# Decay attention with a softplus feed-forward on one core: one block's second product moved behind the others, two pools of PSUM banks joined, q loaded in natural order, another order of instructions

## The chip, the cores and the metric

One core of one Trainium2 chip runs the whole program. The metric is device time in microseconds; lower is better. Engines are called PE (TensorE, with PEld for its weight loads), DVE (VectorE), ACT (ScalarE), POOL (GpSimd) and SP (SyncE, which issues nearly all transfers).

## What is computed

Cut to what matters, the reference is

```python
# q, k, v: (8, 8, 576, 64); f: (8, 8, 576); w_in: (512, 2048); w_out: (2048, 512)
cum = cumsum(log(clip(f, 1e-4, 1)), -1)
scores = q @ k.T / 8 + cum[..., :, None] - cum[..., None, :]      # causal
attn = softmax(scores)                                           # sum + 1e-9
x = (attn @ v) -> (4608 tokens, 512)
h = x @ w_in
out = softplus(h) @ w_out                                        # (4608, 512)
```

All inputs and the output are float32 (the weights reach the kernel as 64-bit words).

## The kernel before

**Precision.** A float32 product is made of three products in a faster format (F32R): each operand is split into a high and a low part, and high times high, high times low and low times high are summed in PSUM. So each operand costs a copy (the high part, `hi_part` or `high`, on ACT or DVE) and a subtraction (the low part, `lo_part` or `low`, on DVE or POOL). The first 14 attention jobs and the first two feed-forward blocks (`plain`) use float32 matmuls directly.

**Work.** There are 70 attention jobs: 14 plain ones for batch 0, and 56 of the split form, one for each head of batches 1 to 7 (`attention`, with `load`, `prepare`, `stat_tile`, `weights`, `output`, `finish`). The 4608 tokens go through the feed-forward in blocks: two of 128 tokens, one of 256, four of 512 (`ffn_block`, blocks 3 to 6; block 6 is tokens 2048 to 2559), and two late blocks of 1024 (`super_blocks`). A 512-token block makes its first product in 16 steps of 12 matmuls (`up_part`, L1506, into a PSUM bank of the tag `h`), softplus on ACT and a split (`gate`), and its second product with 2 of its 4 token tiles at once (`down_part`), the gate's values for the other two tiles going to HBM (`g_d`) and coming back for `second`, the block's tail. Both run through `products`, L1580, and sum up in two banks of the tag `acc`. Tail and normal part are 96 matmuls each.

**Late blocks.** After the last attention job the two late blocks run with a seven-product scheme over quarters of the operands (products P1 to P7 with sums of quarters, instead of eight). First all first products (L2050, 42 matmuls of 512 columns for each of 8 pairs of feature columns and each block); their softplus goes unsplit to HBM (`raw_d`). Then all second products in sets (`down_set` loads, sums and splits; `down_products`, L2387, 42 matmuls of 256 columns for a set; `down_out` joins the seven results). There are 2 blocks x 4 x 4 = 32 sets.

**Order.** Nothing is ordered by hand. Each operation is entered into a `Plan` with its possible engines and a cost for each, what it waits for, and the tags of the buffers that it takes. `Plan.run` then picks, among the next 700 entries, the one that could start first by these costs, less a bonus for its kind (`SOONER`), on the engine that would end it first, with a bias for kind and engine (`RATHER`); this gives each engine its queue. Feed-forward steps are dealt out between the attention units of each job in even shares (`run_ffn`, `share`), so that they last until `REST` = 4 jobs after the last one; with `PAIR` = 1.4 a share is saved up until that much work is due. An operation that is not `loose` takes a buffer of a tag only as the first in that tag's queue. Eight PSUM banks are divided as `att` 4, `h` 2, `acc` 2. `fill_gap` puts dummy matmuls into gaps of PE's plan until the first `acc` bank is taken.

**Operands of an attention job.** `load` brings q and k twice, for the two halves of the partitions. q is brought with its 64-element groups in reverse order (`last_first`), 256 bytes a piece; k as it lies. `prepare` casts them into the operand tile T (L329, ACT or DVE) and subtracts for the low parts (L931). `set_rows` writes constant rows into each of the two T tiles once the plain jobs have read them for the last time.

**Handover.** The late blocks take over the buffers of the attention: operand splits go into the tiles `raw`, T, `vhl`, `ph`, `pl`, `p` and `xl`, sums of weights into `xh` (`place["sums"]`). `xh` and `xl` belong to the running 512-token block until its last `up_part`. The steps of block 6's tail that are left are placed between the first steps of the late blocks (`kept_units`, `left`).

## Time and profile before

| | us |
|---|---|
| median of 3 runs | 1126.86 (1124.36 to 1128.87) |
| the profiled execution | 1123.38 |
| its span on the core | 1121.6 |

The profile is of one execution, which was 3.48 us faster than the median of the three runs. Its span runs from the first to the last recorded instruction; 1.78 us of its time lie around the span.

### The profile page before, as it was taken

The page shows a single profiled execution, that of the slowest core. Times are in us where ns is not written, and L with a number is a line of the kernel's source. Part 1 is how long each engine was busy: PE and PEld are TensorE (multiplying, and loading weights), DVE is VectorE, ACT ScalarE, POOL GpSimd, SP SyncE. Part 2 cuts the span into 40 slices and gives each one's busy share as a digit, 9 for nine tenths or more (in the row PEclk, how much of TensorE's full clock was granted, in tenths as well). Part 3 has the DMA queues.
Part 4 walks back from the last instruction along what each step waited for, and adds up shares of the span by engine and source line. Part 5 has one row for each costly group of instructions (what it writes and reads, how often), then busy time and mean ns, then how long its engine had stood idle before and what let it go on. Part 6 is the DMA issues. An engine that isn't in the chain of part 4 may idle for free.

```text
span 1121.6 us, 21642 instructions
## 1 busy us (share of the span) xinstructions
PE 1101.8 (98%) x6764; PEld 950.3 (85%) x6764; DVE 883.7 (79%) x2445; ACT 811.0 (72%) x2014; POOL 471.6 (42%) x426
## 2 busy tenths in 40 slices
PE   9999999999999999999999999999999999999998
PEld 7777688888888888888888888888888788999998
DVE  7887799887776777878788877886865997998773
ACT  7888789878887888878888888786554665544441
POOL 3423556656663456644655445553000245002111
PEclk9999999999999999999999999999999999999999
DMA  8877676545565566565657646645776776443431
GB/s 224 255 221 229 192 223 182 161 145 176 149 193 173 164 184 194 150 196 153 187 158 204 196 143 203 176 147 161 235 226 189 238 209 196 137 137 122 147 123 57
DMA packets 220866, 200.54 MB, mean 179 GB/s; under 512 B 86384, under 2 KB 189072, under 8 KB 220752
## 3 DMA queue, kind: packets, MB, share of 16 engines
q1 hardware_dynamic: 220728, 199.15, 59.7%
q8 instruction: 53, 0.87, 0.3%
q14 instruction: 61, 0.50, 0.1%
q10 hardware_dynamic: 24, 0.02, 0.0%
HBM read 141.17 MB, written 57.84 MB: 177 GB/s over the span
## 4 chain that ended last, share of the span: by engine, by line
PE 81%; DVE 11%; DMA 3%; ACT 3%; issue 1%; SPq 0%; POOL 0%; DVEq 0%; ACTq 0%; POOLq 0%
PE acc L1580 17%; PE h L1506 14%; PE b L1118 7%; PE late_E L2387 7%; PE late_E L2050 6%; PE o L1265 6%; PE s L976 3%; PE s L977 3%; PE h L1485 2%; PE s L971 2%; PE late_B L2387 2%; PE late_D L2050 2%; PE late_D L2387 2%; PE late_C L2387 2%; PE late_A L2387 2%; PE late_C L2050 1%
## 5 line engine op out<-in xcount | busy, mean ns | idle before, releaser
L1025 ACT ACTIVATE pb<-s,negm 128x288 f32<-128x288 f32 (+5 forms) x272 | 143.9, 531 | 54.4 <-DVE negm L1018 52.6
L981 DVE CUSTOM_DVE_ANT_0 s<-s,cmask 128x448 f32<-128x448 f32 (+6 forms) x320 | 138.2, 435 | 53.5 <-PE b L1118 26.7
L1550 POOL TENSOR_TENSOR gl<-e,gh 128x512 fp32r<-128x512 f32 x72 | 94.7, 1316 | 102.2 <-DVE gh L329 42.9
L931 POOL TENSOR_TENSOR T<-k,T 64x576 fp32r<-64x576 f32 x56 | 80.4, 1436 | 118.4 <-ACT T L329 67.2
L329 ACT CAST ph<-b 64x128 fp32r<-64x128 f32 x224 | 101.8, 490 | 23.7 <-PE b L1118 22.5
L1140 DVE TENSOR_TENSOR pl<-b,ph 128x512 fp32r<-128x512 f32 x168 | 106.4, 662 | 15.0 <-ACT ph L329 14.0
L976 PE MATMUL s<-T 128*128 128x192 f32 (+1 forms) x336 | 99.7, 304 | 4.3 <-ACT p L1025 2.4
L977 PE MATMUL s<-T 68*128 68x192 f32 (+1 forms) x336 | 98.0, 295 | 0.0
L1506 PE MATMUL h<-xh,wl 128*128 128x512 f32 (+1 forms) x320 | 89.5, 374 | 0.0
L1265 PE MATMUL o<-ph,vhl 128*128 128x512 f32 x336 | 87.9, 299 | 0.4 <-DVE pl L1140 0.2
L931 POOL TENSOR_TENSOR T<-q,T 64x576 fp32r<-64x576 f32 x56 | 81.6, 1457 | 15.6 <-ACT T L329 9.9
L1506 PE MATMUL h<-xh,wih 128*128 128x512 f32 (+1 forms) x320 | 81.6, 377 | 0.0
L1118 PE MATMUL b<-halves,pb 128*128 128x128 f32 x512 | 79.8, 273 | 0.0
L1506 PE MATMUL h<-xl,wih 128*128 128x512 f32 (+1 forms) x320 | 79.4, 370 | 0.0
L329 ACT CAST T<-k 128x576 fp32r<-128x576 f32 x112 | 75.2, 673 | 3.8 <-PE s L976 1.7
L903 POOL TENSOR_TENSOR vhl<-vr,vhl 128x384 fp32r<-128x384 f32 x56 | 58.3, 1041 | 44.7 <-DVE vhl L329 19.7
L976 PEld LDWEIGHTS s<-T 128*128 128x128 f32 (+1 forms) x336 | 60.7, 181 | 14.7 <-ACT p L1025 3.1
L1580 PE MATMUL acc<-woh_dt_float32r,gh 128*128 128x512 f32 x176 | 71.9, 409 | 0.0
L1055 DVE TENSOR_SCALAR pb<-pb,rsum 128x576 f32<-128x576 f32 (+2 forms) x86 | 69.8, 823 | 1.1
L1265 PEld LDWEIGHTS o<-ph,vhl 128*128 128x128 f32 x336 | 63.5, 189 | 7.8 <-DVE pl L1140 1.0
L1265 PE MATMUL o<-pl,vhl 128*128 128x512 f32 x224 | 68.5, 345 | 1.0 <-DVE pl L1140 0.8
L1580 PE MATMUL acc<-woh_dt_float32r,gl 128*128 128x512 f32 x176 | 69.3, 394 | 0.0
(747 smaller groups left out, 3358.3 us busy)
## 6 DMA issues: line engine op xcount, KB each, us to landing
wl<-wil_d SPq DMA_DIRECT2D x40, 512.0 KB
raw_d<-e SPq DMA_DIRECT2D x64, 256.0 KB
q<-in_qkT SPq DMA_DIRECT2D x112, 144.0 KB
k<-in_qkT SPq DMA_DIRECT2D x112, 144.0 KB
vr<-in_vR SPq DMA_DIRECT2D x64, 160.0 KB
x_d<-x SPq DMA_DIRECT2D x28, 288.0 KB
g_d<-gh SPq DMA_DIRECT2D x56, 128.0 KB
g_d<-gl SPq DMA_DIRECT2D x56, 128.0 KB
```

What stands on the lines that cost most here:

```text
L329: (e.tensor_copy if hasattr(e, "tensor_copy") else e.copy)(out, in_)
L931: e.tensor_sub(t[rows, i, :], st[x][rows], tb[rows, j, :])
L976: e.matmul(o, qA[:, S - end : S - q0], kA[:, a:z], start=True, stop=False)
L977: e.matmul(o, qB[0:ST, S - end : S - q0], kB[0:ST, a:z], start=False, stop=True)
L981: e.tensor_tensor_reduce(out=box["o"], in0=box["o"], in1=cmask[0:n_q, right - w : right], scale=-0.125, scalar=m0 if i else 3.0e38, op0=AL ...
L1025: e.activation(o, box["o"], AF.Softplus, bias=m1, scale=-1.0, accum_out=acc)
L1118: e.transpose(box["ps"][0 : x.shape[1], at : at + one.shape[1]], x, one)
L1140: e.tensor_sub(box["l"], box["ps"][:, 0:w], box["h"].bitcast(F32))
L1265: e.matmul(boxes[gi]["ps"][0:m, a:z], st["vhl"][:, c, 0:m], pbox[which][:, o : o + z - a], start=gi in fresh and which == "h", stop=gi == ...
L1506: e.matmul(o, l, r, start=m == 0, stop=m == 11)
L1580: e.matmul(st["acc", tt], l, r[fc], start=first and m == 0, stop=last and m == 2,)
L2387: e.matmul(like(o, y), x, y, start=q == 0 and f_ == 0 and m == 0, stop=q == NQ - 1 and f_ == 1 and m == 2,)
```

## The change

- `LATE_DOWN = (6,)`: block 6 no longer makes its second product in the middle. Its softplus goes unsplit to HBM (`whole_keep` into `raw_m`); its gate's split, its 96 + 96 matmuls of L1580, its g_d traffic and its tail are gone. Instead the late stage makes it in 2 x 4 = 8 more sets, ahead of the other 32. The shares of `run_ffn` count 12 instead of 24 matmul groups for such a block.
- `acc` and `att` become one tag `att` with six banks; the two sums of a 512-token block take two of them while they last. The dummy matmuls take one until the first up-projection.
- q is loaded in natural order, 2304 bytes a piece; the reversal of its groups is done by the casts and subtractions of `prepare`, which read q in reverse.
- `PAIR` = 0, many new values in `SOONER` (the plain jobs have their own, marked " early") and `RATHER`, some costs of the planner changed (a shift costs 0.11 us more, the cast of v is counted as fast on DVE, some operations count as using a port that DVE and POOL share).
- `HYB` = 8 lets a number of plain jobs run in the split form from 6 + 8 = 14 on. The first split job is number 14 before as well, so with this value no job changes its form. `set_rows` for one T tile waits for the scores of one plain job instead of two.

```diff
-PLAIN = 0
+HYB = 8
+LATE_DOWN = (6,)
-PAIR = 1.4
+PAIR = 0.0
...
 RATHER = {
-    ("attention.prepare.<lambda>", "ACT"): -1.44,
+    ("attention.prepare.<lambda>", "ACT"): 0.75,
...
-                if "acc" in op.takes:
+                if op is self.stop:
                     self.fill = None
...
-    BUFS = dict(T=2, att=4, h=2, acc=2, fe=4, ph=3, pl=3, ph64=2, gh=LAG + 1, gl=LAG + 1, xh=1, xl=1,
+    BUFS = dict(T=2, att=6, h=2, fe=4, ph=3, pl=3, ph64=2, gh=LAG + 1, gl=LAG + 1, xh=1, xl=1,
+    raw_m = dpool.tile([max(1, len(LATE_DOWN)), 2, 2, WIDE // 256, 2, P, NFP // 2, P], F32, name="raw_m")
...
                 for r in (0, 64):
-                    out = st["q"][r : r + 64].rearrange("p (n t) -> p n t", t=64)
-                    e.dma_start(out=out, in_=last_first(qkT[b, :, heads[0], 0]))
+                    e.dma_start(out=st["q"][r : r + 64, 0 : S - qs], in_=qkT[b, :, heads[0], 0, qs:])
...
             def high(e, i, x, rows):
-                copy(e, t[rows, i, :], st[x][rows])
+                if x == "q":
+                    copy(e, blocks(t[rows, i, 0:nq]), last_first(st[x][rows, 0:nq]))
+                else:
+                    copy(e, t[rows, i, 0:S], st[x][rows])
...
-            if number < nplain + 2:
-                set_rows(number % 2, T0_end[2 * (number % 2)] + T0_end[2 * (number % 2) + 1])
+            if number < nfirst + HYB + 2:
+                set_rows(number % 2, T0_end[number % 2])
...
             a = add(on_act(512, psum=True), raw, after=st["ups"][-1:], takes=("gh",) if plain else ("fe",))
             give("h", [a])
+            if i in LATE_DOWN:
+                m = LATE_DOWN.index(i)
+
+                def whole_keep(e):
+                    for odd in range(2):
+                        to = raw_m[m, odd, u % 2, :, u // 8, :, u // 2 % 4]
+                        e.dma_start(
+                            out=to.rearrange("k p n -> p k n"),
+                            in_=box["g"][:, TB * odd : TB * odd + TB].rearrange("p (k n) -> p k n", n=P),
+                        )
+
+                d = add_dma(whole_keep, 256, 2, after=[a])
+                give("fe", [add(NO_ENGINE, mark, after=[d])])
+                for odd in range(2):
+                    kept_at[NSUPER + m, odd, u] = d
+                return
...
-            tags = ["acc"] * len(tiles)
+            tags = ["att"] * len(tiles)
...
-            downs.append([(down_t, lambda u=u, k=k: down_part(u, k)) for k in range(nk)])
+            downs.append([(down_t, lambda u=u, k=k: down_part(u, k)) for k in range(nk) if not raw_only])
         tail = []
-        if ahead < ntile:
+        if raw_only:
+            pass
+        elif ahead < ntile:
...
-        sets = [(s, k, q) for s in range(NSUPER) for k in range(SUPER // 256) for q in range(NQ)]
+        sets = [
+            (NSUPER + m, k, q) for m in range(len(LATE_DOWN)) for k in range(WIDE // 256) for q in range(NQ)
+        ]
+        sets += [(s, k, q) for s in range(NSUPER) for k in range(SUPER // 256) for q in range(NQ)]
...
-            later = sum(NFC * on_pe(WIDE, 24).cost for x in ready_at.values() for _ in x)
+            later = sum(
+                NFC * on_pe(WIDE, 12 if i in LATE_DOWN else 24).cost for x in ready_at.values() for i in x
+            )
```

## Rows read from the trace of the kernel before

**Rows 1.** The page's first two parts: busy time, share of the span and instructions of each engine; then TensorE's busy tenths and its granted clock (PEclk, tenths of full speed) in 40 equal slices of the span.

```profile
span 1121.6 us, 21642 instructions
...
PE 1101.8 (98%) x6764; PEld 950.3 (85%) x6764; DVE 883.7 (79%) x2445; ACT 811.0 (72%) x2014; POOL 471.6 (42%) x426
...
PE   9999999999999999999999999999999999999998
...
PEclk9999999999999999999999999999999999999999
```

**Rows 2.** Busy time by stage: stretch, its length, busy us (and instructions) of PE, PEld, DVE, ACT and POOL, granted clock, DMA share, GB/s. The stages are: plain float32 attention and feed-forward; the first jobs of the split form; the middle; the handover; the first products of the two late blocks (two rows); their second products (two rows).

```profile
0.00:137.00 137.00, 132.21 (x898) 100.92 (x898) 105.41 (x330) 112.54 (x272) 53.53 (x83) 1.00 0.78 226
137.00:330.00 193.00, 186.45 (x1155) 161.16 (x1155) 164.55 (x495) 160.87 (x432) 119.43 (x94) 1.00 0.59 174
330.00:770.00 440.00, 439.68 (x2553) 378.14 (x2552) 343.89 (x1067) 361.09 (x969) 236.59 (x189) 1.00 0.59 174
770.00:800.00 30.00, 30.00 (x159) 25.32 (x158) 21.08 (x46) 16.98 (x39) 2.84 (x2) 1.00 0.63 199
800.00:860.00 60.00, 60.00 (x267) 49.69 (x266) 36.80 (x68) 28.63 (x51) 1.12 (x1) 1.00 0.75 220
860.00:960.00 100.00, 96.42 (x436) 78.53 (x435) 86.75 (x154) 63.12 (x128) 38.63 (x39) 1.00 0.73 214
960.00:1100.00 140.00, 139.87 (x1166) 139.66 (x1165) 120.03 (x280) 66.41 (x128) 19.48 (x20) 1.00 0.42 131
1100.00:1122.00 22.00, 17.13 (x143) 16.93 (x142) 5.15 (x12) 1.35 (x3) 0.00 (x0) 1.00 0.07 25
```

**Rows 3.** The chain that ended last, in order of time (start us, us, what): a run of the middle form's second product (L1580), a run of the late first product (L2050), and three successive sets of the late second product (L2387).

```profile
786.37 8.21 PE acc L1580 x36
...
806.82 9.52 PE late_E L2050 x42
...
1020.65 1.44 PE late_E L2387 x12
...
1025.69 1.44 PE late_E L2387 x12
...
1030.73 1.44 PE late_E L2387 x12
```

**Rows 4.** Who made PE wait between 137 and 330 us: engine line waited for, us in total, times, the longest.

```profile
PE b L1118 <- ACT p L1025: 2.3, 5, 0.5
PE s L976 <- ACT p L1025: 2.2, 2, 1.9
PE o L1265 <- DVE pl L1140: 1.1, 2, 0.8
```

**Rows 5.** Groups of instructions by line over the whole span: busy us, mean ns of one, and after the second bar the engine's idle time before them.

```profile
L1550 POOL TENSOR_TENSOR gl<-e,gh 128x512 fp32r<-128x512 f32 x72 | 94.7, 1316 | 102.2 <-DVE gh L329 42.9 <-issue 13.6 <-DMA k<-in_qkT 12.4
...
L329 ACT CAST T<-k 128x576 fp32r<-128x576 f32 x112 | 75.2, 673 | 3.8 <-PE s L976 1.7 <-DMA k<-in_qkT 0.9 <-issue 0.6
...
L329 ACT CAST T<-q 128x576 fp32r<-128x576 f32 x56 | 37.9, 676 | 0.5 <-DMA q<-in_qkT 0.4
...
L329 DVE CAST gh<-e 128x512 fp32r<-128x512 f32 x61 | 27.7, 454 | 14.3 <-ACT e L325 7.1 <-POOL vhl L903 3.5 <-DMA vr<-in_vR 1.7
...
L2641 PE MATMUL fill<-cmask 128*128 128x128 f32 x44 | 6.9, 282 | 0.0
```

**Rows 6.** A stretch of the middle in which TensorE is never idle (columns as in Rows 2), and two pieces of the chain that stand at the same place of two jobs, two jobs apart.

```profile
395.00:625.00 230.00, 230.00 (x1347) 198.44 (x1346) 183.09 (x564) 189.99 (x511) 134.62 (x108) 1.00 0.60 178
...
433.63 1.49 PE o L1265 x10
...
456.64 1.49 PE o L1265 x10
```

**Rows 7.** The handover, in order of time: the last up-projection of block 6 (L1506), the last attention product (L1265), the first late product (L2050) and block 6's last second products (L1580) on PE; then on DVE the splits of the late weight sums (L1977) and of the operand T4 (late_xl, L1840).

```profile
758.37 1.07 PE L1506 MATMUL h<-xl,wih 128*128 128x512 f32 x4
...
786.04 0.33 PE L1265 MATMUL o<-ph,vhl 128*128 128x320 f32 x1
...
794.42 0.39 PE L2050 MATMUL late_A<-late_raw,wih 128*128 128x512 f32 x1
...
795.78 0.39 PE L1580 MATMUL acc<-woh_dt_float32r,gh_6b 128*128 128x512 f32 x1
...
787.75 0.76 DVE L1977 TENSOR_TENSOR late_xh<-p,late_xh 128x256 fp32r<-128x256 f32 x2
...
800.10 0.69 DVE L1840 TENSOR_TENSOR late_xl<-late_T,late_xl 128x512 fp32r<-128x512 f32 x1
```

**Rows 8.** Packets of all transfers (the DMA view), the queue that carries them, the issues of the q loads with their duration on the queue (ns min/median/max) from the view of the tile q, and one piece of the chain.

```profile
DMA packets 220866, 200.54 MB, mean 179 GB/s; under 512 B 86384, under 2 KB 189072, under 8 KB 220752
...
q1 hardware_dynamic: 220728, 199.15, 59.7%
...
L886 SPq DMA_DIRECT2D q<-in_qkT x112: 626/645/1491, 95.7 to 743.1; - x112
...
113.10 7.18 DMA sto<-in_w_out
```

**Rows 9.** The memsets of the constant rows of the operand tiles T (line 466, called from set_rows): engine, count, ns min/median/max, first and last start; and what their engine waited for.

```profile
L466 POOL MEMSET T<- x4: 571/571/572, 89.9 to 109.7; 4x576 f32 x4
...
  PE s L971: 1.5, 2
```

More of the change, by code (lines that the diff above doesn't have):

```diff
@@ new lines @@
+    "attention.load.k early": -0.11,
+    "attention.load.q": 0.7,
+    "attention.load32.qk early": 4.58,
+    "attention.load32.rows early": 5.34,
+    "attention.load_quad.<lambda> early": 3.74,
+    "attention.load_v.v early": 0.28,
+    "attention.prepare.decay_rows": 2.88,
+    "attention.split_v.v_hi": -0.39,
+    "attention.split_v.v_hi early": -0.21,
+    "attention.split_v.v_lo": -0.72,
+    "attention.stat_tile.scores": 0.08,
+    "attention.stat_tile.scores early": 2.28,
+    "attention.stat_tile.sums early": 5.04,
@@ new lines @@
+    "attention.stat_tile.weight early": -0.17,
+    "attention.weights.hi_part": 0.04,
+    "attention.weights.keep early": 0.15,
+    "attention.weights.spread": 3.08,
+    "attention.weights.spread early": -0.43,
+    "attention.weights.turn": 0.09,
+    "decay.load early": 3.08,
+    "ffn_block.gate.hi_part": -0.29,
+    "ffn_block.gate.keep": -0.98,
+    "ffn_block.gate.lo_part": -0.38,
+    "ffn_block.gate.raw": -0.54,
+    "ffn_block.gate.raw early": -0.3,
+    "ffn_block.gate.whole_keep": 5.1,
@@ L116 @@
[L116 to L124 removed]
+    ("attention.finish_stats.scale", "ACT"): -1.26,
@@ new lines @@
+    ("ffn_block.gate.lo_part", "POOL"): 0.21,
+    ("load_f64.sign early", "ACT"): -1.9,
+    ("put_out.<lambda>", "ACT"): -0.38,
+    ("split_w_out.hi_part early", "ACT"): 0.46,
+    ("split_w_out.hi_part early", "DVE"): 0.51,
+    ("super_blocks.down_set.split.high", "DVE"): 1.33,
+    ("super_blocks.lay_sums.<lambda>", "POOL"): 0.16,
+    ("super_blocks.lay_sums.low", "POOL"): 1.93,
+    ("super_blocks.lay_w.split.hi", "ACT"): 1.54,
+    ("super_blocks.lay_w.split.hi", "DVE"): 0.19,
+    ("super_blocks.lay_x.less.go", "DVE"): 0.6,
```

230 lines of the change are left out of this document (123 added, 107 removed).

## The prediction, made before the changed kernel was run

> **What bounds the kernel now.** I read the page's first parts first: PE is busy for 98% of the span, in every slice but the last, and its granted clock is full throughout, so the clock is no part of the argument [rows 1]. A busy PE is not yet PE at its peak, so the next view is the table of stages [rows 2]: between 330 and 860 us PE is never idle for more than 0.3 us, and between 960 and 1100 us it rests 0.1 us. Its idle time is 4.8 us before 137 us, 6.6 us from 137 to 330, 3.6 us from 860 to 960 and 4.9 us at the very end, 20 us in all; 6.9 us of dummy matmuls at the start are counted as busy [rows 5]. So the kernel is bound by the sum of PE's work. An edit can gain in two ways only: less work for PE, or less of those 20 + 7 us. An edit that relieves another engine, or a transfer, gains nothing where PE has no gap.
>
> **Part one: block 6's second product moves to the late stage.** It removes 2 x 96 = 192 matmuls of L1580. A run of 36 takes 8.21 us, 0.228 us each [rows 3], so 192 take 43.8 us; by the late first product's pace (9.52 us for 42, 0.227) they would be 43.5. It adds 8 sets. Sets follow each other in 5.04 us (1020.65, 1025.69, 1030.73), which is 42 matmuls at the 0.120 us that 12 in 1.44 us give [rows 3]; the stretch 960 to 1100 has 1166 matmuls in 139.9 us, the same 0.120 [rows 2]. Eight sets: 40.3 us. Net **-3.5 us** (bounds -3.2 and -3.5). The seven-product scheme saves an eighth of the columns, but half of that is lost, because 256 columns in 0.120 us are slower for a column than 512 in 0.228; PEld is busy for 139.7 of those 140 us, so the weight load has become as long as the matmul it should hide behind [rows 2]. DVE is busy for 86% of that stretch, 4.3 us of each 5.04, so sums and splits of the added sets hide behind PE, with 0.7 us to spare; without that cover each set would cost what DVE is late.
>
> The Trainium skill, "TensorE: Matmul & The Clock Gate", section "Back-to-back issue gap", gives a gap of N/2.4 + 2.5 ns for N columns. By it the removed matmuls would be 192 x 0.216 = 41.4 us, the added ones 336 x 0.109 = 36.7 us, and the gain 4.8 us. The rows show longer gaps for both forms, so the page's estimate is not used.
>
> What else goes with block 6: 16 of the 72 gate splits, 0.454 us on DVE and 1.316 us on POOL each [rows 5]; neither engine bounds this stage, so this is costed at nothing, with PE's full work as the cover. SP's queue loses the 28 stores and 14 x 2 loads of the gate's values and gets 32 half stores in their place and later 16 loads; the waits of the late stage on such loads fell on ACT and DVE, not on PE, and I cost them at nothing too.
>
> **Part two: the middle gets shorter, the attention does not.** Between 395 and 625 us PE is never idle; two jobs take 23.0 us, 11.5 for a job, and ACT is busy for 83%, DVE for 80%, POOL for 59% [rows 6], that is 9.5, 9.2 and 6.7 us a job. The shares spread the 43.8 us over jobs 22 to 69 and `REST`, 52 steps, so 0.84 us a job: PE's 11.5 becomes 10.7. Then ACT is at 89%, DVE at 85% (0.15 us of gate casts go). Does that let PE run dry? From below: between 395 and 625 us nothing is lost at 83%. From above: between 137 and 330 us, with ACT at 83% and DVE at 85%, PE is idle for 3.4% [rows 2]; 3.4% of the 396 us left of the middle would be 13.5 us. The jobs in question are those of 395 to 625 with a little less filler between them, so I take a value near the first row: **+1.5 us**. The cast of the operand tiles is 168 casts, 113 us, all on ACT now [rows 5]; the sign of the bias turns, so many will go to DVE. At the 0.454 us of DVE's 512-column cast, 0.51 us for 576, all three of a job would add 1.5 us to DVE's 9.0: 10.5 of 10.7 us. The planner takes the engine that ends first, so I expect a part of them, and no gain of its own.
>
> **Part three: six banks.** Between 137 and 330 us PE waited 2.3 and 2.2 us for ACT's exponentials (L1025) and 1.1 us for DVE [rows 4]. A score's bank is free only after its exponential, so four banks let PE run ahead by less than one job; two more help where no block sums into them, and with them both waits for L1025 can go. A wait of L1118 may also be for the exponential's value, which no bank shortens. Bounds 0 and -6.6 us (the stage's whole idle time); I take **-4 us**, nearly the two waits for L1025. In the middle a 512-token block holds two of the six most of the time, as before, and PE has no idle time there to win. New is that its two sums stand in the attention's queue: what comes later in that queue and is not loose waits until they have their banks. Queued behind are L1118 and L1265, then ACT and DVE; their cover is the filler of the middle.
>
> **Part four: q and the order of the start.** The q loads are 112 issues of 64 rows in 9 pieces, 64512 of the 86384 packets under 512 bytes [rows 8]; they become 7168. SP spends 0.645 us on an issue; the bytes are the same, so I leave that. DMA is busy for 78% of the first 137 us and 59% after [rows 2]. At 113 us the chain stands 7.2 us on a weight load [rows 8], next to q loads; there shorter queues help. The start has 4.8 us of idle time and 6.9 us of dummies, and the order of all plain jobs changes. No row prices an order: below, nothing; above, half of the 11.7, -6 us; against, +4 if it comes out as bad as the idle time it has now. I take **-3 us**. Reading q in reverse costs ACT and POOL the same number of elements (0.676 us a cast): nothing, as they have slack.
>
> **Part five: the handover.** Now block 6's last first product ends at 759 us, and its tail fills PE while the last two jobs drain (last product at 786.0) and DVE lays out the late operands (787.75 to 800.8) [rows 7]. Of the 96 tail matmuls, 36 + 12 come after 786 [rows 3, 7]. Afterwards the filler is first products, and `xh` and `xl` are free only after the last of them; then the sums' splits come (0.42 us each on DVE), one of which the second late product needs. Left over at the end are 4 shares. Blocks 3 to 6 have 4 x 384 matmuls at 0.228 us, 350 us in 52 steps, 6.7 us a share; without the 43.8 us it is 5.9, so 3.4 us of cover less. Bounds: 0 if the order closes it, 8.2 us if the cover of the 36 is gone. I take **+2 us**.
>
> **The sum.** -3.5 + 1.5 - 4 - 3 + 2 = -7.0 us, from 1123.4 of the profiled execution to 1116.4. The median of the runs shown stands 3.5 us above that execution; I carry this over: **1119.9 us**, 0.6% faster.
>
> **Rivals.** (a) *Only the products count.* Waits are not from banks, the start keeps its gaps, middle and handover lose nothing or as much as is won: 1126.9 - 3.5 = 1123.4, no change that can be told (0.5%, 5.6 us, is what a measurement of this kernel can tell). For it: PE is without a gap for three quarters of the span. (b) *Most gaps close.* -3.5, -6.6 and -6 without losses: 1110.8. Against it: nothing in the start's order shows which gap is meant. (c) *ACT or DVE becomes the bound of the middle*, the other side: the shorter jobs meet an ACT at 89% or, with the casts moved, a DVE near its full 10.7 us, and PE rests for 3.4% there as it does at 137 to 330. +13.5 - 3.5 = +10, 1136.9 (1129.9 if the -7 of banks and start come in). It decides from 1.8% idle in the middle on, where gains of 7 us are eaten; for it, the 85% of DVE at 3.4% idle; against, 83% of ACT with none. (d) *The constant rows come too early.* They run on POOL, which waited 1.5 us for scores [rows 9]; with one job's scores as the condition they may be queued before the reads of the T tile end, and what is behind them on that engine waits up to one job, 11.5 us: 1131 at worst.
>
> **How the numbers follow.** Forecast 0.42, (a) 0.34, (b) 0.12, (c) 0.09, (d) 0.03. Faster is the forecast and (b), 0.54; same is (a), 0.34; slower (c) and (d), 0.12. The range runs from 1108, a little beyond (b), to 1131, with (c)'s milder form and (d); it leaves out the rest of (c) and what lies under (b). The forecast's own range is 1115 to 1122.
>
> **What would show it.** Right: 192 fewer matmuls of L1580 and 336 more of L2387, sets still 5.04 us apart; jobs 10.7 us apart in the middle without PE idle; fewer waits for L1025 before 330 us; a gap of up to 3 us near the handover. Wrong: PE idle for over 2% in the middle, with DVE or ACT above 95% (c); sets further apart than 5.1 us; a longer stage before 137 us; more matmul time for a unit of work than now.

## The result, and the profile of the changed kernel

The changed kernel takes 1140.02 us in the median of 4 runs (1136.76 to 1146.17), the kernel before 1127.4 in runs beside it (1124.36 to 1128.87): 1.0119 times as long, 95% interval 1.0081 to 1.0157. The forecast was 1119.9, faster; it came out 1.2% slower. The changed kernel's profiled execution is its slowest run, 1146.17 us with a mean granted clock of 0.989; the other three have 0.993, 0.994 and 0.996 at 1140.23, 1139.81 and 1136.76 us. The kernel before stands at 0.998 to 1.000 in the runs beside the first four experiments and at 0.994 to 1.000 in those beside the others.

The page of the changed kernel, busy time by engine and TensorE's busy tenths and granted clock, which answer to [rows 1]:

```profile
span 1144.4 us, 22047 instructions
...
PE 1111.7 (97%) x6896; PEld 959.9 (84%) x6896; DVE 920.5 (80%) x2587; ACT 758.1 (66%) x1881; POOL 535.4 (47%) x493
...
PE   8899999999999999999999999999999999999998
...
PEclk8799999999999999999999999999999999999999
```

The work is what the change says: PE has 132 instructions more, which is 336 new matmuls less 192 removed less 12 dummies (44 before, 32 now). The span grew by 22.8 us: 12.9 us are idle time of PE (32.7 instead of 19.8), 9.9 are busy time, though 3.5 us of work had gone. The clock row says where the busy time comes from: two of the first slices are no longer at full clock. By stage (columns as in [rows 2]):

```profile
0.00:137.00 137.00, 128.79 (x840) 100.41 (x841) 107.54 (x346) 96.43 (x233) 45.52 (x69) 0.93 0.71 210
137.00:330.00 193.00, 188.02 (x1160) 159.28 (x1158) 164.24 (x512) 153.04 (x414) 139.07 (x115) 1.00 0.57 174
330.00:745.00 415.00, 408.19 (x2402) 348.84 (x2402) 329.91 (x1065) 320.74 (x872) 274.80 (x243) 1.00 0.60 179
745.00:775.00 30.00, 29.13 (x158) 24.45 (x157) 21.74 (x54) 20.25 (x46) 1.91 (x3) 1.00 0.65 192
775.00:835.00 60.00, 60.00 (x266) 49.69 (x265) 40.86 (x77) 23.46 (x40) 8.89 (x11) 1.00 0.78 229
835.00:930.00 95.00, 91.13 (x390) 73.64 (x389) 84.10 (x146) 51.66 (x103) 33.58 (x34) 0.98 0.69 200
930.00:1120.00 190.00, 186.44 (x1526) 184.00 (x1525) 163.10 (x373) 90.55 (x175) 30.17 (x19) 1.00 0.44 132
1120.00:1144.40 24.40, 20.03 (x165) 19.63 (x164) 9.02 (x21) 2.02 (x4) 1.45 (x2) 0.96 0.16 55
```

Three places lost. The start rests 8.2 us before 137 us (4.8 before the change) at a mean clock of 0.93. The middle, 330 to 745 us, rests 6.8 us where it had none to speak of. The late stage, from the last attention job to PE's last product, rests 8.4 us, 3.7 before the change.

**The start.** Five-microsecond stretches of the same profile (columns as above):

```profile
15.00:20.00 5.00, 2.99 (x23) 2.48 (x22) 4.41 (x17) 4.51 (x13) 3.17 (x5) 0.96 0.93 272
20.00:25.00 5.00, 5.00 (x23) 3.84 (x22) 4.33 (x15) 2.73 (x8) 1.41 (x3) 0.50 0.53 162
25.00:30.00 5.00, 5.00 (x26) 4.02 (x25) 2.73 (x13) 2.94 (x8) 0.92 (x1) 0.51 0.44 92
40.00:45.00 5.00, 3.42 (x15) 1.52 (x13) 2.32 (x9) 1.42 (x4) 0.49 (x1) 1.00 1.01 307
45.00:50.00 5.00, 3.17 (x8) 1.55 (x9) 3.80 (x11) 3.60 (x10) 2.10 (x3) 0.69 0.14 43
50.00:55.00 5.00, 5.00 (x18) 3.94 (x17) 2.32 (x13) 1.39 (x3) 1.05 (x2) 0.50 0.51 149
```

PE rests 2.0 us before 20 us and 3.4 us around 45, and after each rest the granted clock is 0.50, that is 1.2 instead of 2.4 GHz, for some 10 us in which PE is busy and does half its work. Why it rests is in the chain that ended last (start, us, what), first ahead of the rest before 20 us, then of that around 45:

```profile
10.58 4.16 DMA sti<-in_w_in
...
15.47 0.44 DVE ti L640
...
17.80 0.19 DVE rsum L1083
...
18.12 0.60 POOL one L354
```

```profile
37.44 7.00 DMA xh_st<-in_w_in
44.46 0.67 ACT ti L637
45.15 0.43 DVE ti L640
...
46.30 0.48 DVE p L354
...
46.83 1.34 PE s L1015 x2
```

At the second rest a 512 KB piece of the weights takes 7.0 us to land; ACT waits for it with the first step of the weights' split (L637), DVE has the second step (L640) next in its queue, and behind it on DVE is the copy `p` that PE waits for. At the first rest it is the same with another piece (`sti`): behind the split's steps on DVE stands a job's `rsum`, and PE waits for what POOL makes of it (`one`). PE is not waiting for the weights, but for small work that stands behind them in two queues. The Trainium skill, "DMA: Bandwidth & Descriptors", section "Anatomy of one DMA — SWDGE (gpsimd) path", gives 2.0 us plus the bytes over 436 GB/s for a transfer that POOL issues, which would make an estimate of 3.2 us for 512 KB. This load is issued by SP, so the trace cannot test that sum: it takes 7.0 us, with the DMA engines fully busy from 40 to 45 us (1.01 in the row above).

ACT's waits for loads in the first 100 us, in the change and then in the kernel before:

```profile
ACT ti L637 <- DMA xh_st<-in_w_in: 3.3, 2, 2.8
ACT ti L637 <- DMA sti<-in_w_in: 2.1, 1, 2.1
ACT to L637 <- DMA xl_st<-in_w_out: 2.0, 1, 2.0
```

```profile
ACT ti L610 <- DMA sti<-in_w_in: 1.2, 2, 0.9
```

7.4 us against 1.2: in the order of before, ACT hardly meets a load that has not landed.

How late the start is by then can be read from the reciprocal of the 14th job, the last of the plain form: first in the change, then in the kernel before.

```profile
122.51 0.18 DVE L1083 RECIPROCAL rsum<-lsum 128x3 f32<-128x3 f32 x1
```

```profile
112.08 0.18 DVE L1039 RECIPROCAL rsum<-lsum 128x3 f32<-128x3 f32 x1
```

It comes 10.4 us later, in a run that is 6 us slower than the change's median.

**The late stage.** It counts from the reciprocal of the last attention job (DVE, start and us; the change, then before) to the end of the span:

```profile
751.84 0.19 DVE L1083 RECIPROCAL rsum<-lsum 128x5 f32<-128x5 f32 x1
```

```profile
776.78 0.19 DVE L1039 RECIPROCAL rsum<-lsum 128x5 f32<-128x5 f32 x1
```

Here 1144.4 - 751.8 = 392.6 us, before 1121.6 - 776.8 = 344.8. Eight sets are 40.3 of the 47.8 more. The added sets are as cheap as forecast, 5.04 us apart on the chain:

```profile
1001.87 1.44 PE late_E L2461 x12
...
1006.91 1.44 PE late_E L2461 x12
```

Of the other 7.5 us, 4.7 are the rests (8.4 against 3.7 us), which lie at the first products and the first sets. The longest of PE's waits there, and the chain at this place:

```profile
PE late_E L2120 <- ACT late_E L354: 2.4, 1, 2.4
```

```profile
882.66 1.43 DVE ws L2291
884.09 0.88 DVE late_r L2021
...
887.83 0.69 DVE late_t L2154
888.54 0.60 ACT late_E L354
889.18 4.62 PE late_E L2120 x12
```

PE needs the bank `late_E`, ACT's copy into it needs `late_t`, and DVE makes `late_t` only after sums of weight quarters (`ws`, `late_r`), which stand ahead of it in its queue.

### The profile page after: what moved, and what is told of

Read it like the earlier page. It is cut to its first block, busy times and chain, and to the rows that moved or that the text cites. A ratio compares the mean times of both kernels' runs of the same rounds, so it can differ in the third digit from the quotient of the medians.

```text
span 1144.4 us, 22047 instructions
## 1 busy us (share of the span) xinstructions
PE 1111.7 (97%) x6896; PEld 959.9 (84%) x6896; DVE 920.5 (80%) x2587; ACT 758.1 (66%) x1881; POOL 535.4 (47%) x493
## 4 chain that ended last, share of the span: by engine, by line
PE 65%; DVE 14%; DMA 8%; ACT 4%; POOL 4%; issue 3%; SPq 2%; DVEq 0%; POOLq 0%; ACTq 0%
PE h L1555 12%; PE acc L1648 9%; PE late_E L2461 7%; PE o L1314 6%; PE b L1166 5%; PE late_E L2120 5%; PE s L1020 3%; PE s L1021 3%; PE late_B L2461 2%; PE late_A L2461 2%; PE late_C L2461 2%; DMA vr<-in_vR 2%; DVE pl L1189 2%; PE late_D L2461 2%; PE late_A L2120 1%
## 5 line engine op out<-in xcount | busy, mean ns | idle before, releaser
L1025 DVE CUSTOM_DVE_ANT_0 s<-s,cmask 128x448 f32<-128x448 f32 (+6 forms) x320 | 134.9, 445 | 18.1 <-PE s L1021 11.5
L1100 POOL TENSOR_SCALAR pb<-pb,rsum 128x320 f32<-128x320 f32 (+2 forms) x96 | 141.8, 1485 | 0.4 <-DVE rsum L1083 0.4
L354 ACT CAST ph<-b 64x128 fp32r<-64x128 f32 (+1 forms) x223 | 101.2, 492 | 32.8 <-PE b L1166 28.7
L1020 PE MATMUL s<-T 128*128 128x192 f32 (+1 forms) x336 | 102.2, 314 | 5.6 <-DVE negm L1062 2.8
L1314 PE MATMUL o<-ph,vhl 128*128 128x512 f32 x336 | 85.2, 291 | 0.5 <-DVE pl L1189 0.5
L1364 DVE TENSOR_TENSOR x<-o,x 64x64 f32<-64x64 f32 x112 | 50.7, 454 | 41.5 <-ACT x L354 39.9
L1100 POOL TENSOR_SCALAR p<-p,rsum 64x64 f32<-64x64 f32 (+1 forms) x99 | 62.2, 639 | 15.9 <-DVE rsum L1083 12.8
L2428 POOL TENSOR_TENSOR late_p<-fY,late_p 128x512 fp32r<-128x512 f32 x7 | 12.0, 1718 | 122.0 <-ACT late_p L354 104.5
L1021 PEld LDWEIGHTS s<-T 68*128 68x128 f32 (+1 forms) x336 | 60.7, 181 | 9.3 <-issue 1.1
L1555 PEld LDWEIGHTS h<-xl,wih 128*128 128x128 f32 x320 | 56.8, 188 | 11.0
```

The lines of the kernel that those rows point to most:

```text
L354: (e.tensor_copy if hasattr(e, "tensor_copy") else e.copy)(out, in_)
L1020: e.matmul(o, qA[:, S - end : S - q0], kA[:, a:z], start=True, stop=False)
L1021: e.matmul(o, qB[0:ST, S - end : S - q0], kB[0:ST, a:z], start=False, stop=True)
L1025: e.tensor_tensor_reduce(out=box["o"], in0=box["o"], in1=cmask[0:n_q, right - w : right], scale=-0.125, scalar=m0 if i else 3.0e38, op0=AL ...
L1100: e.tensor_scalar(a, a, f_, None, ALU.mult)
L1314: e.matmul(boxes[gi]["ps"][0:m, a:z], st["vhl"][:, c, 0:m], pbox[which][:, o : o + z - a], start=gi in fresh and which == "h", stop=gi == ...
```

## The experiments

Two words beforehand. *Order*: which instruction stands where in which queue; `SOONER`, `RATHER` and the costs decide it through the kernel's own plan. *Planned end*: where that plan ends by its own costs: 1092.0 us before, 1090.8 for the change, so that the plan itself promised 1.2 us. One can take the planned order, let every load land 1 us later than the plan counts, and see where it would end then: 16 us later for the kernel before, 34 us later for the change. Those are properties of an order, worked out from the plan, and no times of the chip; they suggested the experiments.

| run | median us (range, runs) | against before, 95% interval | granted clock of its runs |
|---|---|---|---|
| e1_no_late | 1145.6 (1141.82 to 1147.78, 4) | 1.0169, 1.0146 to 1.0191 | 0.990 to 0.996 |
| e3_early_old | 1154.87 (1152.72 to 1162.94, 4) | 1.0268, 1.0230 to 1.0305 | 0.980 to 0.993 |
| e2_old_tables | 1187.05 (1183.26 to 1188.1, 4) | 1.0532, 1.0510 to 1.0554 | 0.973 to 0.979 |
| e5_qrev | 1137.51 (1131.32 to 1141.83, 4) | 1.0096, 1.0060 to 1.0133 | 0.993 to 0.998 |
| f1_dummies | 1137.49 (1136.18 to 1139.4, 4) | 1.0107, 1.0081 to 1.0132 | 0.994 to 0.996 |
| g1_refit | 1119.96 (1116.4 to 1124.45, 9) | 0.9954, 0.9934 to 0.9974 | 0.992 to 0.998 |
| g2_refit | 1123.71 (1121.13 to 1132.05, 12) | 0.9986, 0.9967 to 1.0005 | 0.989 to 0.999 |
| n1_plan_only | 1130.33 (1129.5 to 1133.46, 11) | 1.0043, 1.0030 to 1.0057 | 0.997 to 1.000 |
| g3_padded | 1119.12 (1117.56 to 1120.44, 6) | 0.9939, 0.9918 to 0.9960 | 0.996 to 0.999 |
| h1_before_refit | 1133.25 (1132.82 to 1138.6, 6) | 1.0072, 1.0051 to 1.0093 | 0.992 to 0.997 |
| h2_no_late_refit | 1133.47 (1127.05 to 1138.2, 12) | 1.0052, 1.0033 to 1.0070 | 0.987 to 0.998 |
| h3_banks42_refit | 1127.8 (1124.42 to 1134.06, 12) | 1.0015, 0.9998 to 1.0032 | 0.992 to 1.000 |
| k1_A130G | 1129.21 (1125.62 to 1132.8, 12) | 1.0026, 1.0008 to 1.0043 | 0.989 to 0.998 |
| k2_G140A | 1140.09 (1135.72 to 1146.33, 6) | 1.0121, 1.0091 to 1.0152 | 0.989 to 0.998 |
| k3_A710G | 1129.61 (1125.77 to 1133.46, 12) | 1.0034, 1.0019 to 1.0049 | 0.990 to 0.998 |
| k4_G740A | 1127.48 (1123.79 to 1136.0, 12) | 1.0021, 0.9999 to 1.0043 | 0.987 to 0.999 |

The kernel before has medians of 1125.4 to 1126.2 us beside these runs and 1127.4 beside the change. So the change and g1_refit lie 20 us apart by their medians, and 18.6 by their ratios to it.

### One part undone at a time

**e1_no_late**, the moved product back in the middle, and **e5_qrev**, q loaded reversed again with the order untouched:

```diff
-LATE_DOWN = (6,)
+LATE_DOWN = ()
```

> The changed kernel with LATE_DOWN empty: block 6 makes its second product in the middle again, all else as changed. Theory 1 (start): the start is as slow as in the changed kernel and the products cost 3.5 us more, so about 1143 us. Theory 2 (the middle lost its filler): PE's idle time between 330 us and the handover falls from 6.8 us to under 1 us, which gives 1140 + 3.5 - 6, about 1137.5 us.

```diff
-                    e.dma_start(out=st["q"][r : r + 64, 0 : S - qs], in_=qkT[b, :, heads[0], 0, qs:])
+                    out = st["q"][r : r + 64].rearrange("p (n t) -> p n t", t=64)
+                    e.dma_start(out=out, in_=last_first(qkT[b, :, heads[0], 0]))
...
+                    copy(e, t[rows, i, 0:S], st[x][rows])
```

> The changed kernel with q loaded in reverse order again, in pieces of 256 bytes, and read straight by the casts. Theories 1 and 2 both expect nothing from q itself: within 3 us of the changed kernel, 1137 to 1143 us, the packets under 512 bytes back at about 86000. Rival 3 (reading q in reverse makes casts and subtractions slow or blocks POOL): the time falls by more than 3 us and the casts of q get shorter than 0.6 us on DVE.

Without the moved product the median is 5.6 us above the change's, though their intervals against before overlap: undoing the part brings nothing back. Nor does it price the part, for the values in the tables belong to the structure with it, and the plan of this run ends at 1101.2 us, 10 us later. PE rests 3.8 us from 330 to 745 us, between the two theories.

With q reversed the interval overlaps the change's: the load of q is not told from nothing. The casts of q on DVE do get shorter, 500 ns instead of the 744 that they take when they read in reverse (on ACT 669 and 668), as rival 3 had it; but these are 14 casts, and the time does not show them. Its profiled run (1131.3 us) is of use in another way: all engines have the same order as in the change, PE rests 1.1 us before 20 us instead of 2.0, and the granted clock is full all through the start.

```profile
109.75 0.18 DVE L1083 RECIPROCAL rsum<-lsum 128x3 f32<-128x3 f32 x1
```

The 14th job's reciprocal comes 12.7 us earlier than in the change's profiled run, and 2.3 us earlier than in the kernel before. The loads of q cannot be why: they begin at 90 us. What the change's run has more is two stretches of some 10 us at half clock, about 10 us by their half work, and 2.6 us of rests (5.4 against 2.8). So one order of the start can be ahead of the kernel before or 10 us behind it. The last job's reciprocal comes at 735.6 us instead of 751.8, and the late stage still takes 393.9.

### The old values on the new structure

**e3_early_old** gives the plain jobs the values of before, **e2_old_tables** all operations, with `PAIR` 1.4:

```diff
-        op.sooner = SOONER.get(kind, 0.0)
+        old = self.phase == " early"
+        kind = kind_of(emit) if old else kind
+        sooner, rather = (OLD_SOONER, OLD_RATHER) if old else (SOONER, RATHER)
+        op.sooner = sooner.get(kind, 0.0)
```

> The changed kernel, but the plain jobs (those marked early) take their bonuses and biases from the tables of the kernel before. Theory 1 (the new order of the start is the loss: weight loads land late, PE runs dry between 12 and 60 us and its granted clock falls): job 13 ends its sums at about 112 us instead of 122.5, the clock is 1.00 throughout, and the time falls by 8 to 11 us, to about 1130 us. Theory 2 (the shorter middle is the loss, PE idle for 1.6% there): the start improves but jobs 21 to 69 stand where they stood, so that not more than 3 us are left at the end, about 1137 us or above.

```diff
-PAIR = 0.0
+PAIR = 1.4
...
-        op.sooner = SOONER.get(kind, 0.0)
+        old = True
+        kind = kind_of(emit) if old else kind
+        sooner, rather = (OLD_SOONER, OLD_RATHER) if old else (SOONER, RATHER)
+        op.sooner = sooner.get(kind, 0.0)
```

> The changed kernel with both tables and PAIR of the kernel before: the moved product, six banks, natural q and the planner's new costs stay. If the tables are the loss (theory 1, widened to all stages): the time is that of the kernel before less the 3.5 us of the products, 1122 to 1127 us. If the structure is the loss (theory 2 and the handover): 1136 us or above, with PE idle for over 1% of the middle.

Both are much slower, by 15 and 47 us against the change, and their planned ends are later as well (1113.4 and 1152.7). By the letter the theories that lay the loss on the parts have it (1137 and 1136 us or above), but g1_refit below has the same parts and takes 1120 us, so this is again the order. The old values for the start are no cure: in e3_early_old the 14th job's reciprocal comes at 115.7 us, 6.8 earlier than in the change, but PE then rests 15.1 us between 137 and 330 us (5.0 in the change). What the two show is how large the term is that I had bounded by a few microseconds: the same parts with other numbers in two tables and `PAIR` lie 47 us apart.

### The same instructions, another order

**g1_refit** is the changed kernel with other values in the two tables and nothing else. They were found by changing values at random from the change's own and keeping what made the plan, and the plan with late loads, end earlier.

```diff
-    "attention.load.k": 5.71,
+    "attention.load.k": 0.67,
...
-    "attention.weights.spread": 3.08,
+    "attention.weights.spread": 0.01,
...
-    "super_blocks.down_set.split.high": 2.74,
+    "super_blocks.down_set.split.high": -0.7,
...
```

> The changed kernel with other values in SOONER and RATHER and nothing else: the same instructions, banks, loads and sets in another order. The values were fitted so that the kernel's own plan ends as early as before (1091.1 us planned, 1090.8 with the change's values), and so that the same order still ends early when loads land later than the plan counts: with every load 1 us later the plan of the change's values ends 34 us later (before's kernel: 16 us), that of these values 9 us later. Theory 1, the loss is the order: the change's values place the uses of loads close behind the planned landing, and on the chip loads land later. Then the start keeps PE fed, the granted clock stays at 0.998 or above, the late stage from the last attention job on takes about 385 instead of 392.6 us, and the time is 1113 to 1125 us. Theory 2, the loss is in the parts themselves (shorter jobs in the middle, late stage with more sets and less cover): the middle's 5 to 7 us of idle PE and the late stage's 8 us stay, and the time is 1132 to 1142 us.

1119.96 us: 20 us less than the change, 0.46% less than before, and 0.1 us from the forecast. Theory 1 stands on the time, and the late stage too:

```profile
734.54 0.19 DVE L1178 RECIPROCAL rsum<-lsum 128x5 f32<-128x5 f32 x1
```

1119.0 - 734.5 = 384.5 us. The clock missed: 0.992 to 0.998, where 0.998 or above was expected, so a full clock is not what made the 20 us. The stages of its profiled run:

```profile
0.00:137.00 137.00, 130.01 (x875) 100.28 (x876) 112.11 (x346) 101.73 (x240) 58.64 (x96) 0.96 0.72 220
137.00:330.00 193.00, 191.77 (x1198) 166.50 (x1196) 165.39 (x526) 157.37 (x420) 141.39 (x118) 1.00 0.59 183
330.00:734.50 404.50, 401.32 (x2378) 344.81 (x2377) 328.18 (x1069) 317.62 (x865) 262.71 (x229) 1.00 0.59 179
```

PE rests 1.2 us between 137 and 330 us (6.6 before, 5.0 in the change) and 3.2 to the last job (6.8 in the change). ACT's waits from 137 to 720 us name the load that the change's order is tight on, v: first the change, then g1_refit; the kernel before has no such wait there.

```profile
ACT vhl L354 <- DMA vr<-in_vR: 16.6, 12, 2.8
```

```profile
ACT vhl L449 <- DMA vr<-in_vR: 4.7, 3, 2.1
```

**g2_refit** has values fitted for longer in the same way, **n1_plan_only** values fitted as long for the planned end alone (1090.3 us).

```diff
-    "attention.load.k": 5.71,
+    "attention.load.k": 4.1,
...
```

> The changed kernel with values fitted for longer: planned end 1091.1 us as in g1_refit, 8.4 us later with every load 1 us later (g1_refit 8.8), 11.2 us later with the loads of the first 140 us 2 us later (g1_refit 13.2, the change's values 20.7). If the room that the order leaves for late loads is what decides, it is as fast as g1_refit or up to 3 us faster: 1117 to 1120 us; if g1_refit was a lucky order among many, it is anywhere between 1117 and 1130 us.

```diff
-    "attention.load.k": 5.71,
+    "attention.load.k": 0.36,
...
```

> The changed kernel with values fitted as long as g1_refit's, but for the end of the plan alone, with no regard to loads that land late: planned end 1090.3 us, 0.8 us earlier than g1_refit's; with every load 1 us later it ends 31 us later (the change's values 34, g1_refit 9), with the loads of the first 140 us 2 us later 18 us later (20.7 and 13.2). It differs from the change's order in about as many places as g1_refit does. If the room for late loads decides: 1130 to 1140 us, near the changed kernel's 1140, with idle PE in the start and again in the middle. If any newly fitted order does as well as g1_refit's: 1118 to 1126 us, and the account of late loads falls.

n1_plan_only lands at the edge of what the room for late loads was expected to give, 10 us behind g1_refit with a planned end 0.8 us earlier. But it does so at full clock (0.997 to 1.000), not with a poor start: its profile loses between 137 and 330 us, where PE rests 8.8 us and waits for exponentials and for copies on DVE and POOL; ACT waits 2.6 us for v there, 8.2 from 137 to 720 us. g2_refit is 3.7 us slower than g1_refit though its plan has a little more room. If room for late loads is what decides, it counts for some 10 us here, with 4 us of chance among orders of about the same room. That it decides is argued, not shown: n1_plan_only has hardly more room than the change (31 against 34 us later) and is 10 us faster, and the kernel before, refitted below, gets slower with more room.

### Where in the order it is lost

The four runs of this set use one set of values up to a moment of the plan and the other behind it; A is the change's order, G that of g1_refit.

```diff
-                key = s and (s[0] - op.sooner, op.rank)
+                key = s and (s[0] - op.sooner - op.more * (clock["PE"] >= THEN), op.rank)
...
-        for on in op.on:
+        for on in op.then if op.then and clock["PE"] >= THEN else op.on:
```

> The changed kernel in its own order up to 130 us of the plan and by g1_refit's values from there on; planned end 1092.1 us. Against g1_refit (1120.0) only the start is that of the change. If the 20 us add up from the stages, of which the late one is worth 8 (392.6 against 384.5 us in the two profiles) and the middle 3 to 6 (636.5 to 639.6 against 633.9), the start is worth the other 6 to 9 and this gives 1126 to 1129 us, with the granted clock at 0.996 or below. If the start is worth nothing by itself: 1120 to 1122.

> The reverse: g1_refit's order up to 140 us of the plan, the change's values from there on; planned end 1094.5 us, 3.7 us later than the change's. By the same account the middle and the late stage of the change cost 11 to 14 us over g1_refit: 1131 to 1134 us. If the start is all: 1120 to 1124 us.

> The changed kernel's order up to 710 us of the plan, g1_refit's values from there on; planned end 1090.8 us. Only the late stage is repaired: from the last attention job to the end 384 to 386 us instead of 392.6, and 1131 to 1133 us instead of 1140. If the late stage's loss follows from the state in which the middle hands over, it stays near 392 us, and the time near 1140.

> g1_refit's order up to 740 us of the plan, the change's values from there on; planned end 1090.5 us. Only the late stage is that of the change: 391 to 394 us from the last attention job to the end instead of 384.5, and 1126 to 1129 us. If the late stage's order is not at fault: 1119 to 1121.

The late stage is settled. g1_refit's late part on the change's rest gains 10.4 us (1129.61 against 1140.02), the change's late part on g1_refit's rest costs 7.5 (1127.48 against 1119.96). In the five profiles with the change's order there (the change, e5_qrev, f1_dummies, k2_G140A, k4_G740A) it takes 391.5 to 394.5 us and has PE's wait of 2.4 us for `late_E`; in the four with g1_refit's order (g1_refit, g3_padded, k1_A130G, k3_A710G) it takes 384.0 to 386.6 and the wait is not there. That is 8 us of the 20.

The start is not. The change's start on g1_refit's rest costs 9.2 us (1129.21 against 1119.96), but in k1_A130G's profile the 14th job's reciprocal comes only 3.5 us later than in g1_refit's (114.6 against 111.1 us), and PE rests 7.3 us right behind the cut, where g1_refit rests 1.2:

```profile
137.00:330.00 193.00, 185.68 (x1128) 156.03 (x1127) 165.78 (x497) 148.38 (x402) 132.44 (x111) 1.00 0.56 171
```

k2_G140A missed: 1140.1 instead of 1131 to 1134, no better than the change. Its plan ends 3.7 us later than the change's, PE rests 7.7 us between 137 and 330 us, and its longest waits are new ones:

```profile
PE b L1362 <- POOL pb L1296: 4.1, 3, 3.1
PE late_E L2316 <- ACT late_E L550: 2.4, 1, 2.4
```

So a cut at 130 or 140 us opens rests of its own, and how the 10 to 12 us that are not the late stage's divide between start and middle stays open.

### The rest and the clock

**f1_dummies** puts 16 more dummy matmuls into the change's rest at 16.7 us, **g3_padded** 8 into g1_refit's rest at 36.3 us.

```diff
+            if op.at == 153:
+                self.fill(engines["PE"], 16 * 0.215)
             if eng == "PE" and self.fill:
```

> The changed kernel with 16 more dummy matmuls (2.05 us at full clock) ahead of the product before which PE rested 2.0 us at 16.7 us of the profiled run. Nothing else moves. If the half clock from 20 to 30 us follows from that rest, the granted clock of 20 to 30 us is 1.00 and the median falls by up to 5 us, to 1135 to 1137; the second fall of the clock, 45 to 58 us, stays where its own rest stays. If the half clock there has another cause, the time is 1140 or, by the added dummies, up to 1142.

```diff
+                for _ in range(plan.pad):
+                    e.matmul(box["ps"][:, 0:P], cmask[:, 0:P], cmask[:, 0:P], start=True, stop=True)
```

> g1_refit with 8 dummy matmuls (1.0 us at full clock) ahead of the product at 37.3 us before which PE rested 1.05 us, the last rest before the granted clock fell to half at 40 us in g1_refit's profiled run. If that rest is what the fall follows, the granted clock stays at 0.997 or above in more of the runs and the median falls from 1120 to 1116 to 1119 us; if the fall comes from elsewhere, 1119 to 1121 us.

The stretches of f1_dummies:

```profile
15.00:20.00 5.00, 5.00 (x47) 5.00 (x47) 4.70 (x17) 3.90 (x11) 3.17 (x5) 1.00 0.91 260
20.00:25.00 5.00, 5.00 (x42) 3.88 (x41) 4.53 (x17) 3.66 (x9) 1.75 (x3) 1.00 0.47 159
25.00:30.00 5.00, 4.98 (x44) 4.64 (x43) 3.60 (x16) 3.62 (x12) 0.00 (x0) 1.00 0.80 233
40.00:45.00 5.00, 4.16 (x18) 2.32 (x17) 4.68 (x14) 3.54 (x9) 1.68 (x2) 0.83 0.77 203
45.00:50.00 5.00, 5.00 (x24) 4.75 (x23) 2.54 (x11) 3.34 (x8) 1.07 (x2) 0.50 0.67 194
```

With the rest filled, 20 to 30 us run at full clock. In the other profiles with this start, half clock stands behind this rest where it is 1.6 to 2.5 us long (the change, e1_no_late, k1_A130G, k3_A710G), and not where it is 1.1 (e5_qrev). The median falls by 2.5 us only, which four runs of each don't tell from nothing; a rest of 0.8 us after 40 us is left, with half clock behind it. g3_padded's clock is 0.998 or above in five of six runs (g1_refit: in one of nine); its median is 0.8 us lower, which nine and six runs don't tell from nothing. It is the fastest of all kernels here, 0.6% faster than before.

### The parts, each with an order fitted to it

**h1_before_refit**, **h2_no_late_refit** and **h3_banks42_refit** take all parts, the moved product or the six banks away from g1_refit, and are fitted in the same way.

```diff
-LATE_DOWN = (6,)
+LATE_DOWN = ()
...
-    BUFS = dict(T=2, att=6, h=2, fe=4, ph=3, pl=3, ph64=2, gh=LAG + 1, gl=LAG + 1, xh=1, xl=1,
+    BUFS = dict(T=2, att=4, h=2, acc=2, fe=4, ph=3, pl=3, ph64=2, gh=LAG + 1, gl=LAG + 1, xh=1, xl=1,
```

> The kernel before in its work (block 6's second product in the middle, four and two banks, q reversed by the load, the costs and PAIR of before), with its order fitted anew in the same way and for as long as in g1_refit: its plan ends at 1092.7 us (before: 1092.0), and with every load 1 us later 8 us later (before: 16). It is the control for g1_refit's 1119.96. Theory 1, the parts are worth what was forecast for them (products 3.5 us, banks some us) and the fitting only takes away harm: 1123 to 1127 us, with the late stage at about 345 us. Theory 2, fitting alone brings what g1_refit has over before: 1118 to 1121 us, and then the parts of the change are worth nothing.

> g1_refit without the moved product (LATE_DOWN empty: block 6 makes its second product in the middle again), its order fitted anew, starting from g1_refit's values; planned end 1094.5 us, 3.4 us later than g1_refit's. If the moved product is worth its 192 x 0.228 - 8 x 5.04 = 3.5 us: 1122 to 1125 us. If the eight added sets cost what they save: 1119 to 1121 us.

> g1_refit with banks divided as before, four for attention and two for the sums, its order fitted anew, starting from g1_refit's values; planned end 1094.4 us, 3.3 us later than g1_refit's. If the six banks are worth the 4 us of the forecast: 1122 to 1125 us, and the loss stands between 137 and 330 us, where PE rests 4 to 6 us again instead of g1_refit's 1.2. If they are worth nothing: 1119 to 1121 us.

All three come out slower than either theory had it. The control matters most: the kernel before gets 7.7 us slower by the fitting (1133.25 against 1125.56), though its plan has twice the room for late loads (8 us later against 16). So fitting in this way does not make every structure faster, and room for late loads alone does not foretell the time. It also shows what an order's chance is worth: two orders of the kernel before, with planned ends 0.7 us apart, lie 7.7 us apart.

Between orders fitted alike, the change is worth 1133.3 - 1120.0 = 13 us, or 10 with g2_refit; between the kernel before in its own, faster order and g1_refit, 1126.14 - 1119.96 = 6.2 us. The parts one by one, 13.5 us for the moved product and 7.8 for the banks, are more than the forecast's 3.5 and 4, but with 4 to 8 us of chance at either end none of them is priced by this. For the banks the place does not decide either: between 137 and 330 us h3_banks42_refit rests 8.8 us and g1_refit 1.2, but n1_plan_only, with six banks, rests 8.8 as well, and of h3_banks42_refit's rests only 1.4 us are waits for exponentials.

## Why the prediction was wrong, point by point

**What bounds the kernel** was read rightly: a sum of PE's work with 20 us of gaps. The conclusion from it was one-sided. A kernel with so few gaps has little to gain from an order and much to lose by one, and the change replaces the whole order.

**Part one, the products: right.** 5.04 us a set, 192 matmuls gone, 336 come; the plan without the moved product is 3.4 us longer (1094.5 against 1091.1). The cover by DVE held where the sets follow each other. One reading beside the sum was off: of what an eighth of the columns would save at 0.228 us for 512 (5.5 us), a third is lost to the slower columns, not half.

**Part two, the middle: the sign right, the cause not.** The change rests 6.8 us from 330 to 745 us (1.6%), within the bounds of 0 to 13.5 and above the 1.5 taken; g1_refit rests 3.2. The rival (c) would have had ACT or DVE near their limit: they are busy for 77% and 79% of that stretch, ACT less than before (82%) and DVE about as much (78%). What holds PE up are transfers in the chain of queues: between 330 and 745 us eight of them stand in the chain that ended last, 26.7 us together (before: one, 4.1 us), such as

```profile
475.07 4.58 DMA g_d<-gl
...
702.88 3.96 DMA vr<-in_vR
```

Five are stores of the gate's values, one is a load of v. ACT's waits for v, 16.6 us in 12, are thus a part of it; that they alone are the cause is not shown. I had costed the move of casts between engines by their busy time alone, and the stores at nothing.

**Part three, six banks: right in kind.** The waits for exponentials between 137 and 330 us, 4.5 us in [rows 4], are 0.3 in the change; the stage rests 5.0 us instead of 6.6. In g1_refit it rests 1.2: 5.4 us, beyond the 4 taken. But n1_plan_only has six banks and rests 8.8 there, so that the banks alone do not give it.

**Part four, the start: the step that failed.** It took -3 between -6 and +4, "no row prices an order", with "+4 if it comes out as bad as the idle time it has now". Measured by the 14th job's reciprocal it is +10.4 in the change's profiled run, and -2.3 in e5_qrev's, which has the same order and full clock. So the mechanism that failed is the price of a rest. A rest costs twice: the idle time, and then the half clock, which I had set aside as "no part of the argument" because the profiled run of the kernel before does not show it; half clock is about 10 of the 12.7 us between these two runs. And the rests come from loads: ACT waits 7.4 us for weights in the first 100 us, 1.2 before, with DVE's, POOL's and PE's work behind it. Shorter queues by the natural q could not help there: q's loads begin at 95.7 us [rows 8].

**Part five, the handover: right, but it looked at too little.** The gap is 0.9 us between 745 and 775 us against the 2 taken. The late stage loses its 7.5 us behind it, with the longest wait 114 us later, in an order of DVE's queue, where the prediction's sum has no term. This is the second step that failed, a cost put at nothing, and the one that the swaps show (7.5 to 10.4 us): it took the late stage's order as given because the diff's text there only adds sets. The values in the tables for `super_blocks` had changed too, and they were in the diff.

**The sum.** -7.0 us for the parts is close to what they give in g1_refit's order (-6.2 by the medians, -2.9 to -7.4 by the interval of its ratio). That its time meets the forecast to 0.1 us is luck: it is one order of several with the same planned end, and g2_refit gives -1.9. The missing term is the order that came with the parts: some 20 us, where the bounds had left 7 (+4 against the -3 taken).

**The rivals.** None had this. (d) had the right form, something that stands too early in an engine's queue, but for one pair of memsets: POOL did wait longer there, 5.7 us for scores against 1.5 [rows 9], a small part of what was lost. (c) had the right side and the wrong mechanism.

**What stays open:** how the loss ahead of the late stage divides between start and middle, and how far each single late transfer counts (weights, v, the gate's stores), was not taken apart on the chip; a second buffer for v would show one of them and was not tried. What makes one order better than another of the same planned end is not known either: room for late loads fits the change, g1_refit and g2_refit, and not n1_plan_only and the two orders of the kernel before. The planner's changed costs and `PAIR` were not tried by themselves.

## What to carry to other kernels

When a change comes with a new order, price the order first: list which instructions stand behind a load in each in-order queue, and what lands how late in the trace of before; the span of orders here was 20 us among those with equal planned ends, against 7 us for all the parts together. Fitting a planner's values with loads that land late gave better orders of this structure than the planned end alone (1120 and 1124 against 1130 and 1140 us), but a worse one of the kernel before (1133 against 1126): measure several orders of equal planned end. And compare a structure only with orders fitted to it: with the old values the new structure takes 1187 us, with fitted ones 1120.

## What the runs showed of the hardware

The granted clock of one core alone fell to half, 0.50 or 1.2 GHz, behind short rests of PE in the start: behind 2.0 us before 20 us in the change, not behind 1.1 us in the same place in e5_qrev, and behind 0.8 us after 40 us in f1_dummies; in e3_early_old it did not fall behind a rest of 2.7 us at 32 us. One order can go either way: g1_refit and k4_G740A have the same order up to 740 us and both rest 0.6 us at 7 us, and only in k4_G740A's run does half clock follow, from 10 us on for 13.7 us. So the length of the rest alone does not tell whether it falls. Some 10 us at half clock cost about 5 us. The Trainium skill, "TensorE: Matmul & The Clock Gate", section "What's actually happening", has the throttled clock as the default, which activity releases; the rows agree so far as the clock falls behind rests and comes back while PE is busy.

With one order the time follows the mean granted clock: k4_G740A takes 1124.0 us at 0.999 and 1136.0 at 0.989, and a straight line through its twelve runs gives 0.9 us for each 0.001, through g2_refit's twelve 1.0.

Reading a 128x576 operand with its 64-element groups in reverse makes the cast on DVE take 744 ns instead of 500, while that on ACT takes 668 instead of 669 (the change against e5_qrev).
